# Attention and mixture of products in one kernel: storing x once in fp32, and the order of the last two products

## Chip, cores, metric

One core of one Trainium2 chip runs the whole program. The metric is device microseconds (us) for one execution; lower is better. The kernel before takes 612.06 us, the median of 3 runs (612.0 to 612.1).

## What is computed

Two stages, both fp32. The first is causal attention with a memory term, for B, H, S, D = 4, 8, 576, 64; the second is a gated feed-forward layer on the 2304 tokens (512 columns in, 1536 inside).

```
scores = q @ k.T / sqrt(64), causal
a      = softmax(scores)                       # row sums + 1e-9
local  = a @ v
p      = phi(q)                                # min(exp(q), 1) + relu(q)
mem    = (p @ M_prev) / (p @ z_prev + 1e-6)
x      = g * mem + (1 - g) * local             # g = sigmoid(beta), one per head
x      = x as [2304 tokens, 512]               # heads side by side
out    = (silu(x @ w_gate) * (x @ w_val)) @ w_out
```

## The kernel before

PE is the matrix engine. Its fp32 products are made of halves: an fp32 operand a is kept as a high part ah and a low part al = a - ah, and a product is ah*bh + ah*bl + al*bh. So every operand of a product costs a cast (high) and a subtraction (low). `act`, `dve`, `pool` and `pe` are recorders that keep each engine's work in the order in which the code is written; because a helper issues all of it, nearly every instruction carries line 84 in the profile. SP issues the DMAs in its own queue.

**Attention (lines 568 to 691).** A pair is two heads of one batch; there are 16. The loop over n, 0 to 16, is software-pipelined: pass n, here *turn n*, computes the scores and exponentials of pair n (`ps`, `pl`, `p4` tiles, with row maxima mx and row sums sm) and the transposes, memory term and values of pair n - 1; while it does so the operands of pair n + 1 are split. In a turn

- DVE reads the score banks (ISA rows, with mask and row maximum), makes the reciprocal row sums `rs` (add and reciprocal), evacuates some transposes, and does the memory term.
- POOL multiplies the exponentials by rs and 1 - g: four `ps` (after the first two row blocks) and, at the end of a pass, four `pl` and then one of `p4` (`normal`, line 443). Between them it splits the next pair: `kh`, `qh`, then `ql`, `kl` (lines 297 to 302). On POOL a turn is counted from the four `pl` scalings, which are written at the end of the pass before and run at the turn's start.
- `leave` (541) takes the finished x of a pair out of two PSUM banks (`tr` in the profile): ACT copies the high part to `xh`, DVE subtracts for the low part `xl`, in two pieces of 256 and 320 columns; the second piece is done at the start of the next turn. `d2` (553) stores `xh` and `xl` to two DRAM tensors, `xdh` and `xdl`.
- Four weight thirds are prepared beside attention (EARLY, lines 672 to 682). For the first three, the step that is written at the end of pass n runs at the start of turn n + 1. On DVE it is: turns 4 and 5, 8 and 9, 12 and 13, one op each with one input of 512 columns (clamp, then shift); turns 6, 10, 14, an op with two inputs (`wa<-we,wa`); turns 7, 11, 15, a two-input subtraction (`wgl<-wa,wgh` or like it). Turn 3 has none.

**Experts (lines 923 to 1002).** The tokens form three groups of 768, and w_gate and w_val are cut into 12 column blocks; group by block gives 36 *units*, 0 to 35. A group's x is taken as a 2 x 2 of blocks of 384 tokens by 256 columns, a11, a12, a21, a22, and in units 3 to 35 (`seven`, 879) the two products of a unit are formed from seven block products, p1, p2, p6, p7, p5, p4, p3 in this order, steps 0 to 6. Their operands are x blocks or sums of them, each with a high and a low tile (`xp1h`, `xp1l`, ...): p1 is a11, p2 is a12, p4 is a22 and p6, p7, p5, p3 are combinations, made from an fp32 copy (`xr`, with `xt` and `xm`) by four ops of 768 columns (`sums`, 749). Units 0 to 2 (`eight`) use the blocks themselves. The seven results go through two PSUM banks in turn (`bank`, 847; `s` in the profile), so that a product may start when the bank of the product before last has been read: p1 by ACT (`zp`), p2 by DVE (`zg<-s,zp`), p6 and p7 by ACT, p5 by DVE (`zv<-s,zv`), p4 by DVE (`zh<-s,zh`), p3 by DVE in `weigh`.

`weigh` (833) multiplies the gated half by the value half, ACT casts the result to `uh`, and `halves` (842) writes the subtraction `ul` at the start of the next unit. `weigh(u, 1, g2, v2)` reads two SBUF tiles; `weigh(u, 0, g1, step 6)` reads p3's bank. After each step but the first PE does one of six *lower* products of the unit before (`lower`, 803: three matmuls `tr<-...` with uh, uh, ul of one half), in the order TURN = 3, 4, 5, 0, 1, 2, the first three being those of half 1. `plan[k]` holds DVE and ACT work that is written after step k: the next unit's weight operands (`tt`, `th`, `tl`, `bh`, `bl` from `wr`, each read again from DRAM), weight thirds of later blocks in the first group (`wa`, `wol`), and in the last units of a group the x operands of the next one.

Before the experts, and at each group's end, x comes back by DMA: p1, p2, p7, p4 of the first group and p1, p2, p4 of the others as ready halves (`direct`, 745); for the sums the halves are loaded again and added to fp32 (`add`, 763, four ops of 768 columns, for the second group in units 6 to 9).

Of the kernel before, what the change touches and what calls it, by code (L numbers as in the profile page):

```python
# [9 lines left out]
F32 = mybir.dt.float32  # L10
# [34 lines left out]
def attention_moe(ctx: ExitStack, tc: tile.TileContext, qt, kt_, v, m, beta, wg, wv, wo, out):  # L45
# [9 lines left out]
    xdh = dram.tile([128, NPAIR, NT], F32, name="xdh")  # L55
    xdl = dram.tile([128, NPAIR, NT], F32, name="xdl")
# [109 lines left out]
    xs = {p: [near.tile([128, 2, N2], F32R, name=f"x{p}{part}") for part in "hl"] for p in ("p1", "p2", "p7", "p4")}  # L166

# [88 lines left out]
    with tc.tile_pool(name="sb", bufs=1, reuse_waits="tile") as sb:  # L256
# [69 lines left out]
        class Pair:  # L326
# [239 lines left out]
        ending = lambda: nothing  # L566
        copies = []
        for n in range(NP + 1):
# [10 lines left out]
            low = ending()  # L579
# [5 lines left out]
            low()  # L585
# [80 lines left out]
            ending = old.leave() if old else lambda: nothing  # L666
# [5 lines left out]
            for i, at in enumerate(EARLY):  # L672
# [13 lines left out]
        ending()()  # L686
# [7 lines left out]
    with tc.tile_pool(name="stg2", bufs=1, reuse_waits="tile") as stg2, \  # L694
# [47 lines left out]
        def block(x, t0, i, j):  # L742
            return x[:, 2 * j : 2 * j + 2, t0 + i * N2 : t0 + i * N2 + N2]

        def direct(t0, p, i, j):
            for dst, src in zip(xs[p], (xdh, xdl)):
                SP.dma_start(dst.bitcast(F32), block(src, t0, i, j))

        def sums(t0, here=False):

            got = rot(mbp, "xr", [128, 4, 2, N2], F32, 1)
            at = ((1, 0), (1, 1), (0, 0), (0, 1))
            a21, a22, a11, a12 = (got[:, n] for n in range(4))
# [299 lines left out]
```

## Time and profile before

| | us |
|---|---|
| median of 3 runs | 612.06 |
| the profiled execution | 611.38 |
| its span (first to last recorded work) | 609.6 |
| PE busy | 599.6 (98%) |
| DVE busy | 485.0 (80%) |
| ACT busy | 395.2 (65%) |
| POOL busy | 214.8 (35%) |
| attention, to the first product of the experts | 187.7 |
| one unit of the experts without a stall | 11.48 |

The shares are means over two very different halves: POOL has no work in most of the experts, and in attention it is nearly always busy. Matmuls overlap in the records, so a PE that is shown busy can still lose a few tenths of a microsecond; a loss shows as a longer distance between starts. The granted TensorE clock is full in all of the page's 40 slices.

### The profile page before, as it was taken

Reading aid. Unit: us, or ns where it says so; the run is one execution under the profiler, and the core shown is the slowest. Engines: PE = TensorE matmul, PEld = TensorE weight load, DVE = VectorE, ACT = ScalarE, POOL = GpSimd, SP = SyncE. Lnnn points to the kernel's source line nnn. Section 1 sums busy time; section 2 is a strip of 40 time slices with the busy share of each in tenths; the row PEclk is TensorE's granted clock in tenths of the full one; section 3 lists DMA queues with packets and bytes.
Section 4 is the critical chain, followed back from the end, with each engine's and each line's share of the span. In section 5 each row is a group of like instructions: output and inputs, shape, how many; then the busy total and the mean of one; then the engine's idle time right before and its main releaser. Section 6 shows DMA issues by size and latency. Waiting matters only on the chain.

```text
span 609.6 us, 11282 instructions
## 1 busy us (share of the span) xinstructions
PE 599.6 (98%) x3794; PEld 531.5 (87%) x3794; DVE 485.0 (80%) x1208; ACT 395.2 (65%) x917; POOL 214.8 (35%) x261
## 2 busy tenths in 40 slices
PE   6999999999999999999999999999999999999997
PEld 4878878778788999999899999999999999999996
DVE  6899999999988998898998665665888765665653
ACT  8788888888876777777656654454456654454442
POOL 7999999999963334334320000000000000000000
PEclk9999999999999999999999999999999999999999
DMA  8456756657337657799556622323755622332212
GB/s 250 133 159 178 255 171 204 215 179 216 141 117 277 187 182 239 239 361 282 192 175 208 217 92 70 112 96 115 232 184 177 211 100 69 107 103 69 70 35 103
DMA packets 49321, 102.46 MB, mean 168 GB/s; under 512 B 7024, under 2 KB 17136, under 8 KB 49264
## 3 DMA queue, kind: packets, MB, share of 16 engines
q1 hardware_dynamic: 48832, 101.32, 51.1%
q8 instruction: 30, 0.49, 0.3%
q10 hardware_dynamic: 432, 0.43, 0.2%
q14 instruction: 27, 0.22, 0.1%
HBM read 74.99 MB, written 26.74 MB: 167 GB/s over the span
## 4 chain that ended last, share of the span: by engine, by line
PE 96%; POOL 1%; DMA 1%; issue 0%; DVE 0%; ACT 0%; SPq 0%; ACTq 0%; DVEq 0%
PE s L84 60%; PE tr L84 36%; DMA qr<-in_qt_dram 1%; POOL ps L84 0%; POOL kl L84 0%; SPq L269 0%; ACT g L84 0%; POOL qh L84 0%; DVE rs L84 0%; ACT wa L84 0%; POOL pl L84 0%; DVE mem L84 0%; DVE pl L84 0%; SPq L560 0%; DVE pt L84 0%
## 5 line engine op out<-in xcount | busy, mean ns | idle before, releaser
L84 ACT ACTIVATE zh<-zh 128x384 f32<-128x384 f32 x33 | 17.4, 527 | 74.8 <-DVE zh L84 74.8
L84 POOL TENSOR_SCALAR pl<-pl,rs,og 128x384 f32<-128x384 f32 (+1 forms) x64 | 55.9, 886 | 9.4 <-DVE rs L84 9.4
L84 DVE TENSOR_TENSOR zv<-s,zv 128x384 f32<-128x384 f32 x33 | 18.4, 557 | 51.1 <-PE s L84 45.9
L84 PE MATMUL tr<-woh,ul 128*128 128x512 f32 x144 | 57.3, 398 | 0.0
L84 PE MATMUL tr<-woh,uh 128*128 128x512 f32 x144 | 57.0, 396 | 0.0
L84 PE MATMUL tr<-wol,uh 128*128 128x512 f32 x144 | 56.8, 394 | 0.0
L84 POOL TENSOR_SCALAR we<-we 128x512 f32<-128x512 f32 x32 | 24.9, 780 | 76.8 <-ACT we L84 76.7
L84 ACT ACTIVATE pl<-pl,mx 128x384 f32<-128x384 f32 (+1 forms) x64 | 42.3, 664 | 12.3 <-DVE mx L84 12.3
L84 PE MATMUL tr<-g,vp 128*64 128x320 f32 (+4 forms) x448 | 48.8, 360 | 0.3 <-ACT g L84 0.3
L84 DVE TENSOR_TENSOR tl<-tt,th 128x512 fp32r<-128x512 f32 x66 | 47.7, 723 | 0.0
L84 ACT CAST th<-tt 128x512 fp32r<-128x512 f32 x66 | 41.1, 622 | 9.6 <-DVE tt L84 6.3
L84 PEld LDWEIGHTS tr<-g,vp 128*64 128x64 f32 x448 | 29.4, 137 | 18.0 <-issue 2.3
L84 PE MATMUL s<-kh,qh 64*128 64x128 f32 (+4 forms) x160 | 37.2, 386 | 4.5 <-ACT kh L84 4.0
L84 ACT CAST uh<-zh 128x384 fp32r<-128x384 f32 x36 | 18.5, 513 | 32.6 <-DVE zh L84 32.3
L84 DVE TENSOR_TENSOR zg<-s,zp 128x384 f32<-128x384 f32 x33 | 18.4, 558 | 25.8 <-ACT bh L84 23.5
L84 DVE CUSTOM_DVE_ANT_0 pl<-s,maskp 128x384 f32<-128x384 f32 (+1 forms) x64 | 38.1, 615 | 0.3 <-PE s L84 0.3
L84 DVE TENSOR_TENSOR bl<-wr,bh 128x512 fp32r<-128x512 f32 x66 | 36.3, 550 | 0.0
L84 ACT CAST bh<-wr 128x512 fp32r<-128x512 f32 x66 | 33.9, 513 | 0.0
L84 PEld LDWEIGHTS tr<-woh,ul 128*128 128x128 f32 x144 | 27.1, 188 | 6.8 <-DVE ul L84 0.3
L84 ACT ACTIVATE ps<-ps,mx 128x128 f32<-128x128 f32 (+1 forms) x64 | 28.6, 453 | 6.4 <-DVE mx L84 6.4
L84 POOL TENSOR_SCALAR ps<-ps,rs,og 128x128 f32<-128x128 f32 (+1 forms) x64 | 32.0, 513 | 1.6 <-DVE rs L84 1.2
L84 DVE COPY g<-tr 128x384 f32<-128x384 f32 (+2 forms) x60 | 30.0, 518 | 2.7 <-PE tr L84 1.4
(198 smaller groups left out, 2000.4 us busy)
## 6 DMA issues: line engine op xcount, KB each, us to landing
wr<-wdr SPq DMA_DIRECT2D x24, 512.0 KB, 3.3
wraw<-in_wg_dram SPq DMA_DIRECT2D x12, 512.0 KB, 4.6
wraw<-in_wv_dram SPq DMA_DIRECT2D x12, 512.0 KB, 5.1
wraw<-in_wo_dram SPq DMA_DIRECT2D x12, 512.0 KB, 5.1
wol<-wdo SPq DMA_DIRECT2D x24, 256.0 KB, 2.8
woh<-wdo SPq DMA_DIRECT2D x24, 256.0 KB, 3.1
qr<-in_qt_dram SPq DMA_DIRECT2D x15, 384.0 KB, 3.2
vp<-in_v_dram SPq DMA_DIRECT2D x16, 320.0 KB, 4.1
```

The source lines that it names most:

```text
L84: ins = getattr(eng, name)(*args, **kw)
```

## The change

x is kept once, in fp32. `leave` copies both pieces to one tile `xo` on ACT, and one store a pair goes to one DRAM tensor `xd`; `give`, `d2` and the `xl` subtractions are gone. Where x is used it is loaded as fp32 and split there:

- First group: p1, p2, p7, p4 are loaded into their low tiles in turns 6, 8, 10, 12, and at the end of the two turns after each, ACT casts one half of the tile to the high tile; the subtraction that leaves the low part in place is written a pass later, so that DVE runs the eight of them at the starts of turns 9 to 16, behind the weight op, where there is one.
- `sums` loads four fp32 blocks and adds nothing; of its eight ops of 768 columns four are left.
- Second and third group: p1, p2, p4 are split from `xr` too, p1 and p2 in the group's last unit before them, p4 in the first unit of the group.

In the experts `weigh` reads p3's bank first and the two SBUF tiles second, in all units but the last; the lower products follow in the order 0 to 5 instead of TURN, so that the half that is weighed first is used first; the six lower products after the last unit keep TURN.

```diff
-    xdh = dram.tile([128, NPAIR, NT], F32, name="xdh")
-    xdl = dram.tile([128, NPAIR, NT], F32, name="xdl")
+    xd = dram.tile([128, NPAIR, NT], F32, name="xd")
...
+    where = dict(p1=(0, 0), p2=(0, 1), p7=(1, 0), p4=(1, 1))
+
+    def x_block(t0, i, j):
+        return xd[:, 2 * j : 2 * j + 2, t0 + i * N2 : t0 + i * N2 + N2]
...
-            def give(self, t0, src):
-                c = slice(t0 * 128, t0 * 128 + src.shape[1])
-                act.copy(self.xh[:, c], src)
-                return lambda: dve.tensor_tensor(self.xl[:, c], src, self.xh[:, c].bitcast(F32), op=ALU.subtract)
...
             def leave(self):
                 first, rest = self.av
-                self.xh = rot(sb, "xh", [128, 576], F32R, NX)
-                self.xl = rot(sb, "xl", [128, 576], F32R, NX)
-                self.give(0, first[:, 0:256])()
+                x = rot(sb, "xo", [128, 576], F32, NX)
+                act.copy(x[:, 0:256], first[:, 0:256])
 
                 def ending():
-                    low = self.give(2, rest[:, 0:320])
-                    return lambda: (low(), self.d2())
+                    act.copy(x[:, 256:576], rest[:, 0:320])
+                    SP.dma_start(xd[:, self.pr, self.b * S : self.b * S + S], x)
 
                 return ending
-
-            def d2(self):
-                for dst, src in ((xdh, self.xh), (xdl, self.xl)):
-                    SP.dma_start(dst[:, self.pr, self.b * S : self.b * S + S], src.bitcast(F32))
...
+            for p, at in zip(("p1", "p2", "p7", "p4"), (6, 8, 10, 12)):
+                high, low = xs[p]
+                if n == at:
+                    SP.dma_start(low.bitcast(F32), x_block(ORDER[0], *where[p]))
+                for k in range(2):
+                    if n == at + 1 + k:
+                        act.copy(high[:, k], low[:, k].bitcast(F32))
+                    if n == at + 2 + k:
+                        dve.tensor_tensor(low[:, k], low[:, k].bitcast(F32), high[:, k].bitcast(F32), op=ALU.subtract)
...
-        def direct(t0, p, i, j):
-            for dst, src in zip(xs[p], (xdh, xdl)):
-                SP.dma_start(dst.bitcast(F32), block(src, t0, i, j))
...
-        def sums(t0, here=False):
+        def sums(t0):
 
             got = rot(mbp, "xr", [128, 4, 2, N2], F32, 1)
-            at = ((1, 0), (1, 1), (0, 0), (0, 1))
             a21, a22, a11, a12 = (got[:, n] for n in range(4))
             s1, s = (rot(mbp, name, [128, 2, N2], F32, 1) for name in ("xt", "xm"))
-            tmp = (s, s1)
-            mix = dict(p6=s, p7=a11, p5=s1, p3=a12)
-
-            def load(n):
-                for dst, src in ((got[:, n], xdh), (tmp[n % 2], xdl)):
-                    ld = SP.dma_start(dst, block(src, t0, *at[n]))
-                    follow(ld, last[DVE], "the loads that come before go first", mybir.DependencyClass.Sync)
-
-            def add(n):
-                if here:
-                    h, l = (x.bitcast(F32) for x in xs[("p7", "p4", "p1", "p2")[n]])
-                    dve.tensor_tensor(got[:, n], h, l, op=ALU.add)
-                    return
-                dve.tensor_tensor(got[:, n], got[:, n], tmp[n % 2], op=ALU.add)
-                if n + 2 < 4:
-                    load(n + 2)
+            mix = dict(p1=a11, p2=a12, p6=s, p7=a11, p5=s1, p4=a22, p3=a12)
+
+            def begin():
+                for n, at in enumerate(((1, 0), (1, 1), (0, 0), (0, 1))):
+                    SP.dma_start(got[:, n], x_block(t0, *at))
 
             tt = lambda out, a, b, op: (lambda: dve.tensor_tensor(out, a, b, op=op))
-            work = [lambda n=n: add(n) for n in range(4)] + [
-                tt(s1, a21, a22, ALU.add), tt(s, s1, a11, ALU.subtract), tt(a12, a12, s, ALU.subtract),
-                tt(a11, a11, a21, ALU.subtract),
-            ]
-            return lambda: (load(0), load(1)), work, mix
+            return begin, [
+                tt(s1, a21, a22, ALU.add), tt(s, s1, a11, ALU.subtract),
+                tt(a11, a11, a21, ALU.subtract), tt(a12, a12, s, ALU.subtract),
+            ], mix
...
             rest(5)
-            weigh(u, 1, g2, v2)
-            weigh(u, 0, g1, step(6, "p3", False))
+            ps = step(6, "p3", False)
+            for i, g, v in ((1, g2, v2), (0, g1, ps)) if final else ((0, g1, ps), (1, g2, v2)):
+                weigh(u, i, g, v)
             rest(6)
             return u
...
-                    if left == 0:
-                        plan[2].append(due[7])
-                        plan[3] += spreads(mix, ("h", "p6"))
-                        plan[4] += spreads(mix, ("l", "p6"), ("h", "p7"))
-                        plan[6] += spreads(mix, ("l", "p7"))
-                        arrive = [
-                            (1, spreads(mix, ("h", "p5"))), (2, spreads(mix, ("l", "p5"))),
-                            (3, spreads(mix, ("h", "p3"))), (4, spreads(mix, ("l", "p3"))),
-                        ]
+                if left == 3:
+                    begin, due, mix = sums(follows)
+                    plan[3].append(begin)
+                if left == 1:
+                    plan[2].append(due[0])
+                    plan[5].append(due[1])
+                if left == 0:
+                    plan[1] += spreads(mix, ("h", "p1"))
+                    plan[2] += spreads(mix, ("l", "p1"), ("h", "p2"))
+                    plan[3] += [due[2]] + spreads(mix, ("l", "p2"), ("h", "p6"))
+                    plan[4] += spreads(mix, ("l", "p6"), ("h", "p7")) + [due[3]]
+                    plan[6] += spreads(mix, ("l", "p7"))
+                    arrive = [
+                        (0, spreads(mix, ("h", "p5"))), (1, spreads(mix, ("l", "p5"), ("h", "p4"))),
+                        (2, spreads(mix, ("l", "p4"), ("h", "p3"))), (3, spreads(mix, ("l", "p3"))),
+                    ]
             down = [] if before is None else [
-                lambda j=j, before=before: lower(*before, j) for j in (range(2 * nj) if n <= PLAIN else TURN)
+                lambda j=j, before=before: lower(*before, j) for j in range(2 * nj)
             ]
...
-                before = (unit, seven(ready.pop(n), down, plan, (0, 2, 4) if f else (3, 5, 6)))
-            if not end and left == 0:
-                direct(follows, "p1", 0, 0)
-                direct(follows, "p2", 0, 1)
-                direct(follows, "p4", 1, 1)
+                before = (unit, seven(ready.pop(n), down, plan, (0, 2, 4) if f else (3, 5, 6), n == len(units) - 1))
```

On DVE, at the start of turn 11, the order before is this (`ph` is phi(q), `tr` the bank with x, `s` the score banks):

```order
L84 SCALAR_TENSOR_TENSOR ph_240<-qe_241,ph_240 128x640
L84 TENSOR_TENSOR rs_279<-sm_152,tiny 128x1
L84 RECIPROCAL rs_279<-rs_279 128x1
L84 TENSOR_TENSOR xl_567<-tr_298,xh_566 128x256
L84 TENSOR_TENSOR wgl_1014<-wa_1453,wgh_1013 128x512
L84 ISA ps_271,mx_255<-s_161,maskp 128x128
L84 ISA mx_255 128x1
L84 ISA ps_273,mx_255<-s_162,maskp 128x128
L84 ISA mx_255 128x1
L84 TENSOR_TENSOR xl_567<-tr_303,xh_566 128x320
```

And after:

```order
L83 SCALAR_TENSOR_TENSOR ph_239<-qe_240,ph_239 128x640
L83 TENSOR_TENSOR rs_278<-sm_151,tiny 128x1
L83 RECIPROCAL rs_278<-rs_278 128x1
L83 TENSOR_TENSOR wgl_998<-wa_1430,wgh_997 128x512
L83 TENSOR_TENSOR xp2l<-xp2l,xp2h 128x384
L83 ISA ps_270,mx_254<-s_160,maskp 128x128
L83 ISA mx_254 128x1
L83 ISA ps_272,mx_254<-s_161,maskp 128x128
L83 ISA mx_254 128x1
L83 ISA ps_274,mx_254<-s_152,maskp 128x256
```

Both `xl` are gone, one of them from behind the second pair of score reads, and an `xp2l` subtraction of two SBUF tiles stands directly behind `wgl`.

On DVE, at the end of unit 10 and the first drains of unit 11 (the second `zg` row reads p2's bank in unit 11), before:

```order
L84 TENSOR_TENSOR zh_2647<-s_154,zh_2647 128x384
L84 TENSOR_TENSOR tl_2788<-tt_2786,th_2787 128x512
L84 TENSOR_TENSOR xr_2587<-xr_2587,xm_2589 128x768
L84 SCALAR_TENSOR_TENSOR zh_2647<-zv_2909,zh_2647 128x384
L84 SCALAR_TENSOR_TENSOR zg_2602<-s_153,zg_2602 128x384
L84 TENSOR_TENSOR ul_2665<-zh_2647,uh_2664 128x384
L84 TENSOR_TENSOR ul_2625<-zg_2602,uh_2624 128x384
L84 TENSOR_TENSOR zg_2681<-s_153,zp_2908 128x384
```

After:

```order
L83 TENSOR_TENSOR zh_2610<-s_153,zh_2610 128x384
L83 TENSOR_TENSOR tl_2749<-tt_2747,th_2748 128x512
L83 TENSOR_TENSOR xm_2550<-xt_2549,xr_2548 128x768
L83 SCALAR_TENSOR_TENSOR zg_2567<-s_152,zg_2567 128x384
L83 SCALAR_TENSOR_TENSOR zh_2610<-zv_2870,zh_2610 128x384
L83 TENSOR_TENSOR ul_2589<-zg_2567,uh_2588 128x384
L83 TENSOR_TENSOR ul_2627<-zh_2610,uh_2626 128x384
L83 TENSOR_TENSOR zg_2643<-s_152,zp_2869 128x384
```

The product that reads p3's bank (`zg<-s,zg`) now goes ahead of the one that doesn't (`zh<-zv,zh`), and so do its low half and, with other operands, the 768-column op.

On DVE, in unit 11, from the second weight subtraction to the drain of p4's bank (`zh<-s,zh`), before:

```order
L84 TENSOR_TENSOR xr_2587<-xr_2587 128x768
L84 TENSOR_TENSOR wol_2807<-wa_2040,woh_2806 128x512
L84 TENSOR_TENSOR tl_2905<-tt_2786,th_2904 128x512
L84 TENSOR_TENSOR tt_2786<-wr_2811,tt_2786 128x256
L84 TENSOR_TENSOR zv_2909<-s_154,zv_2909 128x384
L84 TENSOR_TENSOR bl_2907<-wr_2811,bh_2906 128x256
L84 TENSOR_TENSOR xp6l<-xm_2589,xp6h 128x384 x2
L84 TENSOR_TENSOR zh_2742<-s_153,zh_2742 128x384
L84 TENSOR_TENSOR tl_2905<-tt_2786,th_2904 128x512
```

After:

```order
L83 TENSOR_TENSOR xp1l<-xr_2548,xp1h 128x384 x2
L83 TENSOR_TENSOR wol_2768<-wa_2015,woh_2767 128x512
L83 TENSOR_TENSOR tl_2866<-tt_2747,th_2865 128x512
L83 TENSOR_TENSOR tt_2747<-wr_2772,tt_2747 128x256
L83 TENSOR_TENSOR xr_2548<-xr_2548 128x768
L83 TENSOR_TENSOR xp2l<-xr_2548,xp2h 128x384 x2
L83 TENSOR_TENSOR zv_2870<-s_153,zv_2870 128x384
L83 TENSOR_TENSOR bl_2868<-wr_2772,bh_2867 128x256
L83 TENSOR_TENSOR xp6l<-xm_2550,xp6h 128x384 x2
L83 TENSOR_TENSOR xr_2548<-xr_2548,xm_2550 128x768
L83 TENSOR_TENSOR zh_2703<-s_152,zh_2703 128x384
L83 TENSOR_TENSOR tl_2866<-tt_2747,th_2865 128x512
```

Four subtractions (`xp1l`, `xp2l`, two each) and a second op of 768 columns now stand ahead of `zh<-s,zh`.

## Rows read from the trace of the kernel before

**Rows 1.** The page's first part: busy us (share of span) and instructions.
```profile
PE 599.6 (98%) x3794; PEld 531.5 (87%) x3794; DVE 485.0 (80%) x1208; ACT 395.2 (65%) x917; POOL 214.8 (35%) x261
```
**Rows 2.** Windows view, turns 4 to 14: window, length, busy of each engine, PEclk, DMA, GB/s.
```profile
47.06:168.11 121.05, 121.05 (x1115) 97.36 (x1113) 113.49 (x430) 103.51 (x294) 116.54 (x143) 1.00 0.62 195
```
**Rows 3.** Timeline of POOL: start, us, instruction [idle before <-releaser].
```profile
35.89 3.24 POOL L84 TENSOR_SCALAR pl<-pl,rs,og 128x384 f32<-128x384 f32 x4 [0.41 <-DVE rs L84]
...
47.06 3.46 POOL L84 TENSOR_SCALAR pl<-pl,rs,og 128x384 f32<-128x384 f32 x4 [0.52 <-DVE rs L84]
...
57.97 3.46 POOL L84 TENSOR_SCALAR pl<-pl,rs,og 128x384 f32<-128x384 f32 x4 [0.41 <-DVE rs L84]
...
112.90 3.73 POOL L84 TENSOR_SCALAR pl<-pl,rs,og 128x384 f32<-128x384 f32 x4 [0.41 <-DVE rs L84]
...
124.05 3.73 POOL L84 TENSOR_SCALAR pl<-pl,rs,og 128x384 f32<-128x384 f32 x4 [0.41 <-DVE rs L84]
...
128.56 0.67 POOL L84 TENSOR_SCALAR kh<-kr 128x576 fp32r<-128x576 f32 x1
...
133.35 1.43 POOL L84 TENSOR_TENSOR kl<-kr,kh 128x576 fp32r<-128x576 f32 x1
```
**Rows 4.** Timeline of DVE in turns 3 and 11.
```profile
37.69 0.49 DVE L84 TENSOR_TENSOR xl<-tr,xh 128x320 fp32r<-128x320 f32 x1
...
124.77 0.42 DVE L84 TENSOR_TENSOR xl<-tr,xh 128x256 fp32r<-128x256 f32 x1
...
125.11 0.71 DVE L84 TENSOR_TENSOR wgl<-wa,wgh 128x512 fp32r<-128x512 f32 x1
...
128.86 0.38 DVE L84 TENSOR_TENSOR rs<-sm,tiny 128x4 f32<-128x4 f32 x1
...
134.45 0.34 DVE L84 TENSOR_TENSOR rs<-sm,tiny 128x4 f32<-128x4 f32 x1
```
**Rows 5.** Waits of ACT: waited for, us in total, times, longest.
```profile
ACT xh L84 <- PE tr L84: 5.7, 12, 0.5
```
**Rows 6.** Chain of waits, units 7, 11 and 12: start, us, piece.
```profile
267.29 2.33 PE s L84 x12
...
314.20 2.23 PE s L84 x12
...
325.83 2.08 PE s L84 x12
```
**Rows 7.** Timeline of PE, unit 7, the step from p1 to p2.
```profile
268.00 0.34 PE L84 MATMUL s<-xp1h,bl 128*128 128x384 f32 x1
268.31 0.44 PE L84 MATMUL s<-xp2h,bh 128*128 128x384 f32 x1
268.59 0.34 PE L84 MATMUL s<-xp2l,bh 128*128 128x384 f32 x1
268.77 0.34 PE L84 MATMUL s<-xp2h,bl 128*128 128x384 f32 x1
```
**Rows 8.** Timeline of DVE and ACT, units 10 and 11.
```profile
313.18 0.95 DVE L84 TENSOR_TENSOR xr<-xr,xm 128x768 f32<-128x768 f32 x1
...
316.54 0.56 DVE L84 TENSOR_TENSOR zg<-s,zp 128x384 f32<-128x384 f32 x1 [0.28 <-PE s L84]
...
322.20 0.92 ACT L84 CAST xp6h<-xm 128x384 fp32r<-128x384 f32 x2
...
322.75 1.03 DVE L84 TENSOR_TENSOR xp6l<-xm,xp6h 128x384 fp32r<-128x384 f32 x2
...
323.69 0.55 DVE L84 TENSOR_TENSOR zh<-s,zh 128x384 f32<-128x384 f32 x1
...
326.72 0.55 DVE L84 TENSOR_TENSOR ul<-zh,uh 128x384 fp32r<-128x384 f32 x1
```
**Rows 9.** Timeline of PE, the first matmul of units 12 and 24.
```profile
325.67 0.34 PE L84 MATMUL s<-xp1h,bh 128*128 128x384 f32 x1
...
463.43 0.34 PE L84 MATMUL s<-xp1h,bh 128*128 128x384 f32 x1
```
**Rows 10.** Timeline of DVE, unit 23 and the start of unit 24.
```profile
459.52 0.56 DVE L84 TENSOR_TENSOR zv<-s,zv 128x384 f32<-128x384 f32 x1 [1.19 <-PE s L84]
...
461.26 0.55 DVE L84 TENSOR_TENSOR zh<-s,zh 128x384 f32<-128x384 f32 x1
...
464.34 0.55 DVE L84 TENSOR_TENSOR ul<-zh,uh 128x384 fp32r<-128x384 f32 x1
```

More of the change, by code (lines that the diff above doesn't have):

```diff
@@ L565, in attention_moe @@
         nothing = lambda *args: None
-        ending = lambda: nothing
+        ending = nothing
         copies = []
@@ L578, in attention_moe @@
                 old.turns()
-            low = ending()
+            ending()
             while copies:
@@ L584, in attention_moe @@
             reads[0](1)
-            low()
             if n == 0:
@@ L665, in attention_moe @@
                     cur.weighed(((4, 0),))
-            ending = old.leave() if old else lambda: nothing
+            ending = old.leave() if old else nothing
             if n + 2 < NP:
@@ L877, in eight, with seven @@
             return u
-        def seven(w, down, plan, away_at):
+        def seven(w, down, plan, away_at, final):
             def step(n, p, start, before=None):
@@ L915, in attention_moe @@
         first = units[0][0]
-        for p, i, j in (("p1", 0, 0), ("p2", 0, 1), ("p7", 1, 0), ("p4", 1, 1)):
-            direct(first, p, i, j)
         before = None
@@ L948, in attention_moe @@
                 if f == 0:
-                    _, due, mix = sums(t0, True)
-                    for k, some_ in enumerate(((0,), (1,), (2, 4), (3,))):
-                        plan[k] += [due[i] for i in some_]
+                    begin, due, mix = sums(t0)
+                    begin()
+                    plan[2].append(due[0])
+                    plan[3].append(due[1])
                 if f == 1:
-                    for k in range(3):
-                        plan[k].append(due[5 + k])
-                    for k, p in ((0, "p5"), (2, "p6")):
-                        plan[k] += spreads(mix, ("h", p))
+                    for k, i, p in ((0, 2, "p5"), (2, 3, "p6")):
+                        plan[k] += [due[i]] + spreads(mix, ("h", p))
                         plan[k + 1] += spreads(mix, ("l", p))
@@ L963, in attention_moe @@
                 follows = ORDER[ORDER.index(t0) + 1]
-                if t0 == first and left in (5, 4, 3):
-                    if left == 5:
-                        begin, due, mix = sums(follows)
-                        begin()
-                    plan[5].append(due[5 - left])
-                if not plain:
-                    if left == 3 and t0 != first:
-                        begin, due, mix = sums(follows)
-                        plan[3].append(begin)
-                    if left == 2:
-                        for k, work in zip((5,), due[3:]) if t0 == first else zip((2, 4, 6), due):
-                            plan[k].append(work)
-                    if left == 1:
-                        for k, work in zip((1, 3, 5), due[4:]) if t0 == first else zip((1, 2, 4, 6), due[3:]):
-                            plan[k].append(work)
-                    if left == 0:
-                        plan[2].append(due[7])
-                        plan[3] += spreads(mix, ("h", "p6"))
-                        plan[4] += spreads(mix, ("l", "p6"), ("h", "p7"))
-                        plan[6] += spreads(mix, ("l", "p7"))
-                        arrive = [
-                            (1, spreads(mix, ("h", "p5"))), (2, spreads(mix, ("l", "p5"))),
-                            (3, spreads(mix, ("h", "p3"))), (4, spreads(mix, ("l", "p3"))),
-                        ]
```

5 lines of the change are left out of this document (2 added, 3 removed).

## The prediction

> **What bounds the kernel now.** The page's first part comes first: PE is busy 599.6 of 609.6 us [rows 1]. Matmuls overlap, so short waits hide inside that busy time, and the two halves have to be read one by one.
>
> *Attention.* Turns 4 to 14 of the loop over pairs last 121.05 us; PE counts as busy throughout, POOL is busy 116.54 us [rows 2]. A turn begins on POOL with the four scalings of pl, and before them POOL waits 0.41 us for rs [rows 3]. 11 x 0.41 = 4.51, and 116.54 + 4.51 = 121.05: POOL waits for nothing else. So a turn is as long as POOL's work plus 0.41 us, and the others keep POOL's pace. Now see what lengthens that work. The four scalings take 3.24 us in turn 3, 3.46 in turns 4 and 5, 3.73 in turns 10 and 11, and the turns follow: 47.06 to 57.97 is 10.91 us, 112.90 to 124.05 is 11.15 [rows 3]. By the code, what differs at this place is the weight preparation on DVE: none in turn 3, a one-input op of 512 columns in turn 4, a two-input op in turns 10 and 11, as wgl with 0.71 us [rows 4]. The other way round, rs of 128.86 ends at 129.24 with kh (129.23), that of 134.45 at 134.79 with kl (134.78) [rows 3, 4]. DVE ops with both inputs in SBUF and POOL's ops take turns. The xl subtractions are in every turn; they read PSUM and one SBUF tile, and POOL's 3.24 us of turn 3 (35.89 to 39.13) contain one at 37.69 [rows 3, 4]: they do not hold POOL up.
>
> The Trainium skill, "SBUF — State Buffer", section "Who interferes with whom", says the same in general: a VectorE instruction with two SBUF inputs contends with a GpSimd instruction that reads SBUF, one with a single SBUF input outside the 2-port modes does not, and whoever is first holds the port for its whole instruction. The rows agree on who contends, and not quite on the price: by the rule the 0.71 us of wgl would cost POOL 0.71, the rows show 0.49. With the rule's price the sum below would be 0.5 us higher. It speaks against this change, which puts two-input subtractions where one input was PSUM.
>
> *Experts.* The chain of waits is PE's own matmuls. Its pieces of 12 matmuls (p1 and p2) take 2.08 us, but 2.33 in units 7 to 10 and 2.23 in unit 11 [rows 6] (the first of the long ones, that of unit 11 and a short one): 4 x 0.25 + 0.15 = 1.15 us. Inside, the first matmul of p2 starts 0.31 us after its predecessor, not 0.17 [rows 7]. Its bank was last read by the unit before, by the zg product, which stands on DVE behind a 768-column add (0.95 us, as at 313.18) [rows 8] and the other product.
>
> **The change part by part.**
>
> *Stores.* In turns 2 to 16 DVE loses both xl, 0.34 us (124.77 to the next start at 125.11) and about 0.40 [rows 4], and SP one store. Neither is in POOL's work or its 0.41 us, so I take no gain; rival 1 has the other end. ACT copies the same bits as fp32: nothing.
>
> *Splitting x for the first group.* Eight casts come to ACT in turns 7 to 14, between the two copies of x. There ACT waits 5.7 us in 12 turns, 0.48 each [rows 5]; a cast of 384 columns costs 0.46 (two in 0.92) [rows 8]. In turns 10 and 14 a weight op fills that gap already and ACT is 0.46 later; it waits on DVE next. Nothing.
>
> Eight subtractions come to DVE at the starts of turns 9 to 16, from two SBUF tiles. Their like, xp6l, takes 1.03 for two and its follower starts 0.94 after [rows 8], so 0.47 each in the queue. They stand directly behind the weight op (the first order listing). A lone op of 0.71 costs POOL 0.49 (3.73 - 3.24), so 0.22 of one is hidden; an op that follows at once has nothing left to hide in. Low end 0.55 - 0.22 = 0.33, high end 0.55, and 0.47 is nearest to what is in the queue. Turns 9 to 14: 6 x 0.47 = **+2.8** (2.0 to 3.3). In turns 15 and 16 no further pair is split and POOL's work is short: +0.1 (0 to 0.3).
>
> *Loads.* Four loads in turns 6 to 12 in place of eight; later four per group for fourteen. No DMA is in the chain of either half. The loads of a group now wait in SP's queue until DVE and ACT have read the tile, with weight loads behind them; I count 0, up to 0.3.
>
> *Experts, units 6 to 10.* The adds of high and low are gone. Unit 10 keeps a 768-column op there, but the zg product, which frees the bank, now goes ahead of the other one. The stalls go: **-1.15** (at least -0.9). Elsewhere there was no such stall, and the new order of the two products has nothing to give. The last unit keeps its order.
>
> *Unit 11, where the second group is made ready.* p1, p2 and p4 came by DMA as halves; now they are split. Ahead of DVE's zh add (the drain of p4's bank) stand four more subtractions, 4 x 0.47 = 1.88, and a 768-column op that was in unit 10, 0.87: 2.75 us. DVE's visible wait there is 0.28 [rows 8]; the rest, 2.45 to 2.5, is delay. The zh add ended at 323.69 + 0.55 = 324.24, and p1 of the next unit started at 325.67 [rows 8, 9]: 1.43 of room. PE stalls 2.45 - 1.43 = 1.0. Then the first ul: it ended near 327.27, now 329.7; PE wants it as third matmul of the first lower product, 2.08 + 0.46 after p1, at 326.67 + 2.54 = 329.2. Another 0.45. **+1.45** (0.5 to 2.4: at the low end DVE has more short waits to fill, at the high end nothing gives).
>
> *Unit 23* has the same work without weight words. DVE waits 1.19 us before zv [rows 10], so of 2.75 some 1.5 remains. Room up to p1: 463.43 - 461.81 = 1.6 [rows 9, 10], no stall. The first ul, 464.89 before, comes at 466.4; wanted at 463.43 + 2.54 = 465.97: **+0.4** (0 to 1).
>
> *Sum:* 2.8 + 0.1 - 1.15 + 1.45 + 0.4 = +3.6 us. The profiled execution took 611.38 us (span 609.6); 611.38 + 3.6 = 615.0. The median of the runs, 612.06, is 0.68 higher, so **615.7 us**.
>
> **The rivals.**
>
> *1. DVE sets the pace of attention.* DVE is busy 113.49 of 121.05 us [rows 2]. If the xl were on the path, turns 4 to 8 would gain 0.74 each and turns 9 to 14 0.74 - 0.47 = 0.27: 3.7 + 1.6 = 5.3, and the sum would be -5.3 + 0.7 = -4.6: 607.5 us. A smaller form, 0.1 to 0.2 a turn from PE's short waits, gives 610 to 611. Against it: POOL's account closes without DVE's share, and turn 3, with all its xl, has the shortest scalings.
>
> *2. The subtractions cost POOL nothing* because POOL's lateness is made up, if DVE, now earlier elsewhere, has rs ready sooner and the 0.41 us shrink. Then only the experts count: +0.7, 612.8; with unit 11 half covered, 612.0. Against it: rs becomes ready after kl has begun (134.45 against 133.35) [rows 3, 4], so it would have to come 1.1 us sooner.
>
> *3. Turns lose more than POOL's work.* Turn 3 lasts 11.17 us (35.89 to 47.06), though its scalings are the shortest; by its work it should last 10.69. If such half microseconds come to three or four of turns 9 to 14, because DVE's queue is now later at the start of the turn and its rs meets POOL's next op, the time is 617.5 to 618. For it: turn 3 shows that it occurs. Against: once in 11 turns.
>
> *4. The reordered products decide nothing:* with the adds gone the stalls would go anyway. It changes no time; it says which edit has the -1.15.
>
> **How the numbers follow.** The forecast has 0.6, rival 1 0.12, rival 2 0.18, rival 3 0.1. A measurement tells 0.2%, 1.2 us, from no change: 610.8 to 613.3. The forecast's low ends together are 2.0 - 1.15 + 0.5 + 0 = +1.35, 613.4, just above that; its high ends 3.3 + 0.3 + 0.3 - 0.9 + 2.4 + 1 = +6.4, which need not meet, and two thirds of the way up from the middle to there is 617.5. Slower: the forecast but for 0.03 and rival 3, 0.67. Same: rival 2 without its fast edge and a little of the forecast, 0.19. Faster: rival 1 and that edge, 0.14. To leave out no more than 0.2 the range reaches down into rival 2: 611.5 to 617.5.
>
> **What would show it.** POOL's four scalings should take 3.9 to 4.2 us in turns 9 to 14 and stay at 3.46 and 3.73 in turns 4 to 8; turn starts 11.3 to 11.6 us apart there. If they stay at 10.9 to 11.15, that step is wrong. The pieces of 12 matmuls in units 7 to 11 should all take 2.08. In unit 12 PE should stand before p1 and before the third matmul of the first lower product; in unit 24 before the latter alone. If turns 4 to 8 get shorter, DVE had a part in the pace, and rival 1 is right.

## The result, and the profile after

The changed kernel takes 615.88 us (median of 6 runs) beside 612.03 us of the kernel before on the same chip; the ratio is 1.0067, 95% interval 1.0054 to 1.0080. It is slower, and 615.7 was forecast. The profiled execution took 615.79 us with a span of 614.0, against 611.38 and 609.6.

The page's first part, busy us, share of the span and instructions, answers to [rows 1]:

```profile
PE 600.1 (98%) x3794; PEld 529.6 (86%) x3794; DVE 473.6 (77%) x1184; ACT 400.9 (65%) x937; POOL 218.3 (36%) x261
```

DVE does 11.4 us less work than before and the kernel is slower: DVE's total was not what bounds it. The windows view of the same eleven turns as in [rows 2] (window, length, busy of PE, PEld, DVE, ACT, POOL, PEclk, DMA share, GB/s):

```profile
46.91:170.45 123.54, 122.88 (x1115) 97.74 (x1113) 113.07 (x414) 106.31 (x301) 118.05 (x144) 1.00 0.51 155
```

The eleven turns take 123.54 us, 2.49 more, and POOL is busy 1.51 more. POOL's timeline at the starts of turns 4, 5, 8, 9, 10 and 11 and the first scalings of ps in turn 4 (start, us, instruction, [idle before]) answers to [rows 3]:

```profile
46.91 3.39 POOL L83 TENSOR_SCALAR pl<-pl,rs,og 128x384 f32<-128x384 f32 x4 [0.52 <-DVE rs L83]
...
52.84 1.96 POOL L83 TENSOR_SCALAR ps<-ps,rs,og 128x128 f32<-128x128 f32 x4 [0.40 <-ACT ph L83]
...
58.22 3.40 POOL L83 TENSOR_SCALAR pl<-pl,rs,og 128x384 f32<-128x384 f32 x4 [0.50 <-DVE rs L83]
...
91.68 3.38 POOL L83 TENSOR_SCALAR pl<-pl,rs,og 128x384 f32<-128x384 f32 x4 [0.41 <-DVE rs L83]
...
102.50 3.78 POOL L83 TENSOR_SCALAR pl<-pl,rs,og 128x384 f32<-128x384 f32 x4 [0.41 <-DVE rs L83]
...
113.69 4.03 POOL L83 TENSOR_SCALAR pl<-pl,rs,og 128x384 f32<-128x384 f32 x4 [0.41 <-DVE rs L83]
...
125.15 4.04 POOL L83 TENSOR_SCALAR pl<-pl,rs,og 128x384 f32<-128x384 f32 x4 [0.41 <-DVE rs L83]
```

Before, the scalings of turn 9 were these:

```profile
102.04 3.46 POOL L84 TENSOR_SCALAR pl<-pl,rs,og 128x384 f32<-128x384 f32 x4 [0.41 <-DVE rs L84]
```

Two things are to be seen. From turn 9 on the four scalings take 3.78 and 4.03 us where they took 3.46 and 3.73 (that row and [rows 3]): that is the forecast step. And turn 4 lasts 11.31 us (46.91 to 58.22) instead of 10.91, with *shorter* scalings and a new wait of 0.40 before ps: that was not forecast.

The stretches side by side, from POOL's pl starts in attention and from the first matmuls of units in the experts (us; the forecast is the term of the prediction):

| stretch | before | after | difference | forecast |
|---|---|---|---|---|
| to the start of turn 4 | 47.06 | 46.91 | -0.15 | 0 |
| turns 4 and 5 | 21.78 | 22.64 | +0.86 | 0 |
| turns 6 to 8 | 33.20 | 32.95 | -0.25 | 0 |
| turns 9 to 14 | 66.07 | 67.95 | +1.88 | +2.8 |
| from there to the first product of the experts | 19.62 | 19.87 | +0.25 | +0.1 |
| unit 1 | 12.52 | 13.26 | +0.74 | 0 |
| stalls at p2 in units 7 to 11 | 1.15 | 0 | -1.15 | -1.15 |
| units 11 and 12, without that | 22.96 | 24.51 | +1.55 | +1.45 |
| units 23 and 24 | 22.96 | 23.54 | +0.58 | +0.4 |
| sum | | | +4.31 | +3.6 |

The other units take the same time in both, 11.48 us from unit 3 on.

In the experts, the chain of waits in units 10 and 11 (start, us, piece) shows that the pieces [rows 6] at 2.33 have lost their stall. The piece of 30 matmuls is the one of 12, two lower products and two more products run together, 2.08 + 2 x 0.70 + 2 x 1.04 = 5.56 us:

```profile
305.05 5.56 PE s L83 x30
...
316.53 2.10 PE s L83 x12
...
327.52 0.87 DVE xr L83
328.39 0.47 DVE zh L83
```

The last two are the forecast of unit 11: zh, the drain of p4's bank, stands behind a 768-column op. It begins 11.86 us after the unit's first piece (328.39 - 316.53), where it was 9.49 [rows 6, 8]: 2.37 later, 2.45 to 2.5 were forecast. On PE (timeline, the first matmul of p3 and of unit 12's p1, and the third matmul of the first lower products of units 12 and 24 with the one ahead of it):

```profile
326.31 0.45 PE L83 MATMUL s<-xp3h,bh 128*128 128x384 f32 x1
...
328.91 0.45 PE L83 MATMUL s<-xp1h,bh 128*128 128x384 f32 x1 [0.58 <-DVE zh L83]
...
331.36 0.40 PE L83 MATMUL s<-wol,uh 128*128 128x512 f32 x1
331.85 0.50 PE L83 MATMUL s<-woh,ul 128*128 128x512 f32 x1
...
469.67 0.40 PE L83 MATMUL s<-wol,uh 128*128 128x512 f32 x1
470.18 0.50 PE L83 MATMUL s<-woh,ul 128*128 128x512 f32 x1
```

PE stands before p1 and then before the matmul that needs the first ul (0.49 and 0.51 us after its predecessor instead of 0.24), where the prediction put it.

Unit 1 was not forecast. The chain of waits from the end of attention on:

```profile
192.16 0.61 POOL we L83
192.77 6.07 DMA xr<-xd
198.83 1.15 issue
199.98 0.06 DVE xt L83
200.04 0.81 issue
200.85 0.56 DVE zh L83
201.41 0.04 issue
201.46 5.84 PE s L83 x30
```

The loads of x for the sums are let go at 192.77 and land 6.07 us later, in a stretch where the DMA engines are full (windows view, 192 to 202 us: DMA share 1.04, 388 GB/s). DVE's first sum, xt, waits for them, and zh of unit 0, which drains the bank for the second product of unit 1, is queued behind xt. Before, those sums were made from halves that lay in SBUF.

### The profile page after: what moved, and what is told of

Its sections match the earlier page's. It is cut to its first block, busy times and chain, and to the rows that moved or that the text cites. A ratio compares the mean times of both kernels' runs of the same rounds, so it can differ in the third digit from the quotient of the medians.

```text
span 614.0 us, 11191 instructions
## 1 busy us (share of the span) xinstructions
PE 600.1 (98%) x3794; PEld 529.6 (86%) x3794; DVE 473.6 (77%) x1184; ACT 400.9 (65%) x937; POOL 218.3 (36%) x261
## 4 chain that ended last, share of the span: by engine, by line
PE 88%; DVE 5%; DMA 2%; ACT 2%; issue 1%; POOL 1%; SPq 0%; ACTq 0%; DVEq 0%; POOLq 0%
PE s L83 54%; PE tr L83 34%; DMA xr<-xd 1%; DMA qr<-in_qt_dram 1%; DVE rs L83 1%; DMA kr<-in_kt_dram 0%; DVE xr L83 0%; ACT g L83 0%; DVE zh L83 0%; DVE mem L83 0%; DVE zg L83 0%; DVE xp7l L83 0%; DVE xp6l L83 0%; DVE pl L83 0%; DVE tt L83 0%
## 5 line engine op out<-in xcount | busy, mean ns | idle before, releaser
L83 POOL TENSOR_SCALAR pl<-pl,rs,og 128x384 f32<-128x384 f32 (+1 forms) x64 | 58.1, 921 | 9.6 <-DVE rs L83 9.6
L83 POOL TENSOR_SCALAR we<-we 128x512 f32<-128x512 f32 x32 | 26.7, 836 | 74.1 <-ACT we L83 73.8
L83 ACT CAST uh<-zg 128x384 fp32r<-128x384 f32 x36 | 18.5, 514 | 37.8 <-DVE zg L83 37.7
L83 DVE SCALAR_TENSOR_TENSOR zg<-s,zg 128x384 f32<-128x384 f32 x36 | 20.0, 556 | 17.4 <-PE s L83 17.4
```

The source lines that it names most:

```text
L83: ins = getattr(eng, name)(*args, **kw)
```

## Experiments

Kernels without a ratio ran once; a few tenths between such times mean nothing, and their traces are what counts.

### The order of the last two products, undone and alone

Undone in the changed kernel (a_old_order), and put alone into the kernel before (b_new_order):

```
-            ps = step(6, "p3", False)
-            for i, g, v in ((1, g2, v2), (0, g1, ps)) if final else ((0, g1, ps), (1, g2, v2)):
-                weigh(u, i, g, v)
+            weigh(u, 1, g2, v2)
+            weigh(u, 0, g1, step(6, "p3", False))
...
-    for j in range(2 * nj)
+    for j in (range(2 * nj) if n <= PLAIN else TURN)
```

> The changed kernel with only the order of the last two products and of the lower products put back. If the order is what frees p2's bank (my step), units 7 to 11 show PE stalls at p2 again, 0.1 to 0.25 us each, wherever a 768-column op stands in the unit before (in this plan units 10 and 11), so 0.2 to 0.5 us in all, and the rest of the 1.15 us stays away since the adds are gone. By rival 4 nothing comes back: all pieces of 12 matmuls stay at 2.08. Attention is unchanged in either case (experts start at 190.3).

> The kernel before with only the new order of the last two products and of the lower products. The adds of high and low stay. If the order frees the bank, the five pieces of 12 matmuls in units 7 to 11 go from 2.33 and 2.23 to 2.08: -1.15 us, 610.9. By rival 4 (the adds are the cause and order decides nothing) it stays at 612.0, with 2.33.

Undone: 616.13 us. Units 7 to 10 stay at 11.48 us; the chain of waits there and in unit 11:

```profile
270.44 2.08 PE s L83 x12
...
281.92 2.08 PE s L83 x12
...
316.36 2.10 PE s L83 x12
```

No stall comes back in units 7 to 11. Units 12 and 24 lose 0.69 and 0.68 instead of 0.49 and 0.50, now at p2's first matmul.

Alone: 610.66 us beside 611.62, ratio 0.9983 (0.9973 to 0.9992). The chain in units 7 and 8:

```profile
267.46 5.56 PE s L84 x30
...
278.94 5.59 PE s L84 x30
```

The stalls go here too, but for 0.03 us a unit; the experts are 1.06 us shorter. So either edit removes the 1.15 us, and with both the second has nothing left to do: in this change rival 4 is right, the order decides only 0.38 us in units 12 and 24, and by itself it is worth a microsecond.

### The eight subtractions beside attention, left out

```
-                    if n == at + 2 + k:
-                        dve.tensor_tensor(low[:, k], low[:, k].bitcast(F32), high[:, k].bitcast(F32), op=ALU.subtract)
```

> The changed kernel without the eight subtractions beside attention: the low halves of the first group's x are left as the whole x, so the output is not the reference's. Theory (two-input DVE work holds POOL up): the four scalings of pl in turns 9 to 14 fall from 3.78 and 4.04 to 3.39 and 3.65, each of these turns by 0.39, turns 15 and 16 by little; experts start 2.3 to 2.6 us earlier, at 187.7 to 188.0, and the time is about 613.4. The long turns 4 and 5 (11.31 and 11.33) stay. Rival (DVE's queue, not POOL, is the path): the scalings keep their length and PE's turns fall by 0.47.

614.86 us. POOL's timeline, pl of turns 9, 10, 12 and 13, and ps of turn 12:

```profile
102.96 3.37 POOL L83 TENSOR_SCALAR pl<-pl,rs,og 128x384 f32<-128x384 f32 x4 [0.41 <-DVE rs L83]
...
113.72 3.64 POOL L83 TENSOR_SCALAR pl<-pl,rs,og 128x384 f32<-128x384 f32 x4 [0.42 <-DVE rs L83]
...
135.79 3.37 POOL L83 TENSOR_SCALAR pl<-pl,rs,og 128x384 f32<-128x384 f32 x4 [0.41 <-DVE rs L83]
...
141.71 1.95 POOL L83 TENSOR_SCALAR ps<-ps,rs,og 128x128 f32<-128x128 f32 x4 [0.40 <-ACT ph L83]
...
147.11 3.38 POOL L83 TENSOR_SCALAR pl<-pl,rs,og 128x384 f32<-128x384 f32 x4 [0.51 <-DVE rs L83]
```

The scalings fall by 0.40, as expected, and turns 9, 10, 11 and 14 by 0.40 to 0.43. But turns 12 and 13 get *longer* without the subtraction, 11.32 and 11.30 instead of 11.20 and 11.19, with the wait of 0.40 before ps that turn 4 has. Together -1.44 in turns 9 to 14 instead of -2.4; a subtraction costs 0.40 where it costs anything. Turns 9 to 14 still last 66.51 us, 0.44 more than before: of the +1.88 of the table only 1.44 is the subtractions', the rest comes with xl's going (next section).

### xl left out of the kernel before

```
-                return lambda: dve.tensor_tensor(self.xl[:, c], src, self.xh[:, c].bitcast(F32), op=ALU.subtract)
+                return lambda: None
...
-                for dst, src in ((xdh, self.xh), (xdl, self.xl)):
+                for dst, src in ((xdh, self.xh), (xdl, self.xh)):
```

> The kernel before without the subtractions for xl (both stores take xh, so the low half of x is wrong). Theory: attention gains next to nothing from it. By what the changed kernel's trace shows, the scalings of pl get 0.07 shorter, so turns 6 to 14 gain 0.07 each, but kh then ends just before rs is ready in turns 4 and 5 and these become 0.4 longer: experts start between 187.2 and 188.2 (187.73 before). By rival 1 (DVE sets the pace) each of turns 4 to 14 is 0.3 to 0.74 shorter, and the experts start at 180 to 184.

> The kernel before without the xl subtractions again (the low half of x is wrong), timed: open is whether taking xl away costs time or whether turn 4 of the kernel before is itself at the edge, so that the single profile misled. Theory (the shorter scalings let kh end just before rs arrives, in turns 4, 5, 12 and 13): 0.5 to 1.2 us slower than the kernel before, ratio 1.001 to 1.002, the spread of the kernel before wider than its own. By the prediction's step: no change. By rival 1: 5 us faster.

Both profiles agree to 0.05 us: turns 4, 5, 12 and 13 last 11.3 us, the others of 4 to 14 0.05 to 0.11 less than before. The first product of the experts starts at 188.80 in the first, 1.07 later than in the profile of before. Timed, the ratio is 1.0006 (0.9997 to 1.0014; 612.29 beside 611.89): no difference that can be told. Rival 1 wanted 5 us less. What lies between the two answers is seen in turn 4, kh and qh on POOL and rs on DVE. Before:

```profile
51.30 0.67 POOL L84 TENSOR_SCALAR kh<-kr 128x576 fp32r<-128x576 f32 x1
51.94 0.73 POOL L84 TENSOR_SCALAR qh<-qr 128x640 fp32r<-128x640 f32 x1
...
51.92 0.10 DVE L84 TENSOR_TENSOR rs<-sm,tiny 128x4 f32<-128x4 f32 x1
```

After:

```profile
51.07 0.68 POOL L83 TENSOR_SCALAR kh<-kr 128x576 fp32r<-128x576 f32 x1
51.71 0.73 POOL L83 TENSOR_SCALAR qh<-qr 128x640 fp32r<-128x640 f32 x1
...
51.78 0.67 DVE L83 TENSOR_TENSOR rs<-sm,tiny 128x4 f32<-128x4 f32 x1
52.48 0.18 DVE L83 RECIPROCAL rs<-rs 128x4 f32<-128x4 f32 x1
```

rs adds 1e-9 to four row sums, an op of 0.10 us with two SBUF inputs. Before, it arrives 0.05 us ahead of kh's end (51.97) and gets in at once. After, it arrives 0.03 us behind kh's end (51.75): qh has the turn, rs waits it out (0.67 us), and ps waits for rs. The row of ps at 52.84 names ph as what ended its wait. But ps starts 0.18 us after the end of rs's reciprocal (52.66), just as pl at 47.06 before follows its own by 0.18, and without the add (below) the wait is gone.

So the scalings that got 0.07 us shorter without xl cost 0.4 us a turn; why they got shorter is not shown. Before stands at this edge itself: in the profiles of b_two_sbuf and b_two_psum below, whose turns 3 to 8 are the same code, rs arrives 0.03 to 0.04 ahead of kh's end, misses, and turns 4 and 5 take 11.37 to 11.38 us. So the +0.86 of the table is partly luck of the profile of before; of the profiles with the add, turns 4 and 5 were long in every one without xl, and in two of four with it. The 0.05 us alone does not decide either. In turn 3 of the profile of before rs also arrives 0.05 us ahead of kh's end (40.58), and it misses:

```profile
39.89 0.69 POOL L84 TENSOR_SCALAR kh<-kr 128x576 fp32r<-128x576 f32 x1
...
40.53 0.75 DVE L84 TENSOR_TENSOR rs<-sm,tiny 128x4 f32<-128x4 f32 x1
```

### Two more subtractions, from SBUF or from PSUM

In the kernel before, behind the first xl of turns 9 to 16; the control has `first[:, 0:256]` (the PSUM bank) in place of the first input:

```
                 self.give(0, first[:, 0:256])()
+                if 7 <= self.n <= 14:
+                    junk = rot(sb, "junk", [128, 256], F32, 1)
+                    for _ in range(2):
+                        dve.tensor_tensor(junk[:, 0:256], self.xh[:, 0:256].bitcast(F32), self.xl[:, 0:256].bitcast(F32), op=ALU.subtract)
```

> The kernel before with two more DVE subtractions of 128x256 behind the first xl at the starts of turns 9 to 16, each from two SBUF tiles into a tile that nobody reads. Theory (two-input SBUF work on DVE holds POOL up): 0.33 us each in the queue, so the four scalings of pl grow by 0.5 to 0.7 us in turns 9 to 14 and so do the turns; experts start about 3 to 4 us later, near 191.3. Rival (POOL is free of it, DVE's queue is the path): the scalings stay at 3.46 and 3.73.

> The control of the run with two SBUF inputs: the same two DVE subtractions of 128x256 in the same place, but one input is the PSUM bank that holds x. Theory: the scalings of pl stay within 0.1 of 3.46 and 3.73 and the experts start at 187.7 to 188.5. If DVE's queue were the path, these two would cost as much as the SBUF ones, 3 to 4 us.

621.69 and 619.91 us, far more than expected of either. POOL's pl at turn 9 with SBUF inputs:

```profile
103.69 3.89 POOL L84 TENSOR_SCALAR pl<-pl,rs,og 128x384 f32<-128x384 f32 x4 [0.41 <-DVE rs L84]
```

and with PSUM, pl and ps of turn 9:

```profile
103.58 3.37 POOL L84 TENSOR_SCALAR pl<-pl,rs,og 128x384 f32<-128x384 f32 x4 [0.41 <-DVE rs L84]
...
109.85 1.95 POOL L84 TENSOR_SCALAR ps<-ps,rs,og 128x128 f32<-128x128 f32 x4 [0.77 <-ACT qe L84]
```

The scalings do what the theory says: 3.45 becomes 3.89 with SBUF inputs, and 3.37 with PSUM ones. But the two ops also make DVE later: in turn 9 rs of ps comes 5.62 us after the start of pl with SBUF inputs and 5.77 with PSUM ones, where before it came after 4.65. POOL waits for it in turns 9 to 14, 0.76 to 1.00 us with PSUM inputs (turns of 11.7 to 12.2 us) and 0.40 to 1.09 with SBUF ones (11.8 to 12.7); where qe is named as releaser, as above, the reciprocal of rs again ends 0.17 us before ps.

So most of what these runs lost, some 8 of 10 us, is DVE's queue, and only the 1.8 us between them is what the SBUF inputs add: up to that rs DVE has little slack, 0.26 us in turn 9 before (rs at 106.69, kh ends at 106.95). In the change rs of turn 9 comes after 4.79 us, hardly later: the two xl, 0.74 us a turn, left DVE's queue as the subtraction of 0.47 came in. The prediction counted xl's going as nothing; by these sums it was worth having as cover for the subtraction, though no run has the subtraction and xl together.

### rs without its add

A row sum holds an exp(0), so 1e-9 is below its last bit, and the reciprocal can be taken at once. First in ps alone, then everywhere, in the changed kernel; then everywhere in the kernel before, with the new order of products:

```
-                if by is None:
-                    dve.tensor_tensor(rs, self.sm[:, c : c + n], tiny[:, 0:n], op=ALU.add)
-                else:
+                if by is not None:
...
-                    dve.reciprocal(rs, rs)
+                    dve.reciprocal(rs, self.sm[:, c : c + n])
```

> The changed kernel with rs of the first two row blocks (the ps scalings) taken without the add of 1e-9, all other adds kept. Theory (turns 3, 4 and 5 are long because this add, with two SBUF inputs, comes just after kh has ended and has to wait until qh is done): these three turns fall from 11.15, 11.31 and 11.33 to about 10.75, 10.9 and 10.9, the others stay, POOL keeps its 0.41 us before pl; experts start 1.2 us earlier, at 189.1. Rival (the long turns come from something else, such as ACT or a load): no turn changes.

> The changed kernel with rs taken as the reciprocal of the row sum itself, the add of 1e-9 (a DVE op with two SBUF inputs) left out; a row sum holds an exp(0), so 1e-9 is below its last bit. Theory (the add waits for POOL's running op and POOL then waits for rs): turns 3, 4 and 5 lose their extra 0.4 us, POOL's wait before pl goes from 0.41 to 0.1 or less in every turn, so 14 turns get 0.3 to 0.4 shorter; experts start 5 to 6.5 us earlier, at 184 to 185.5, time 609.5 to 611. Rival (POOL's 0.41 us is the way from ACT's last exponential through rs, whatever rs is made of): only the add's own 0.15 us go, 2 us in all.

> The kernel before with the new order of the last two products and with rs without the add of 1e-9. Theory: 610.7 of the new order, less 13 turns of 0.3 to 0.4 and 0.4 for turn 3, so 605 to 606.5. Rival (the wait is the way through rs): 608.5.

In ps alone (614.69 us): turns 3, 4 and 5 fall from 11.14, 11.31 and 11.33 to 10.25, 10.78 and 10.75, POOL's 0.41 us before pl stay in nearly all turns. At the start of turn 3 this execution is 1.5 us late, as is the one of a_units below (1.4), whose attention is unchanged; from there to pl of turn 16 it is 2.2 us shorter. The long turns came from this add.

Everywhere (611.96 us): POOL's 0.41 us vanish, turns 4 to 8 take 10.6 to 10.8 us, the experts start at 186.30, 4.0 earlier, where 5 to 6.5 were expected. One turn went the other way, 12.97 us. DVE's ph and POOL's four pl there:

```profile
130.86 3.96 DVE L83 SCALAR_TENSOR_TENSOR ph<-qe,ph 128x640 f32<-128x640 f32 x1
```

```profile
131.33 2.82 POOL L83 TENSOR_SCALAR pl<-pl,rs,og 128x384 f32<-128x384 f32 x4
```

ph, two SBUF inputs, 0.80 us elsewhere, is ready at 130.86 while kl runs, and ends at 134.82, 0.67 after the last of pl (134.15). At four boundaries between POOL's ops POOL went on and DVE did not. In the kernel before, ph goes into the gap that POOL's wait for rs leaves: in turn 4 it starts at 46.80, pl at 47.06.

In the kernel before: 606.73 us beside 611.78, ratio 0.9925 (0.9911 to 0.9938), the fastest of all here; its runs reach from 605.35 to 609.13. In its profile, that of the run at 605.35, no ph was held for as long. Whether one was in the run at 609.13 is not shown.

### The experts' queue on DVE

In the changed kernel, xt behind zh in unit 0, and the two ops of 768 columns of units 11 and 23 a unit earlier, into tiles of their own:

```
-                    plan[2].append(due[0])
-                    plan[3].append(due[1])
+                    plan[3] += due[0:2]
...
-                tt(a11, a11, a21, ALU.subtract), tt(a12, a12, s, ALU.subtract),
+                tt(d7, a11, a21, ALU.subtract), tt(d3, a12, s, ALU.subtract),
...
-                    plan[2].append(due[0])
-                    plan[5].append(due[1])
+                    for k, work in zip((1, 2, 4, 5), due):
+                        plan[k].append(work)
```

> The changed kernel with two edits in the experts: in unit 0 the first 768-column add (xt) is written after zh's drain, and for the second and third group the two ops of 768 columns that stand in the last unit write tiles of their own, so that they can be done one unit earlier. Theory: unit 1's bank wait came from zh queued behind xt, which waits for the load of x; unit 1 goes from 13.26 back to 12.52 us. In units 11 and 23 1.74 us less stands ahead of zh, and of the 1.54 and 0.58 us of stall most goes: units 11, 12, 23 and 24 take 11.5 to 11.7. Together 2.3 to 2.9 us less in the experts. Rival (the wait in unit 1 is PE's or the load's own, not DVE's order; the stall in unit 11 is from the four subtractions alone): unit 1 stays at 13.2, unit 11 loses at most half. Attention is unchanged.

614.58 us. Unit 1 takes 12.52 us, units 11, 12, 23 and 24 11.81, 11.48, 11.48 and 11.48: 2.53 us less. The rest, 0.33, is a p2 stall: its bank waits for zg behind the ops that now stand in unit 10. The time of the run shows only half of it, since its attention ends 1.3 us later than in the profile after; the kernel before, run beside it, took 613.07 us.

### All mends together

> The changed kernel with all mends together: rs without the add of 1e-9 everywhere, xt behind zh in unit 0, and the two ops of 768 columns one unit earlier. Theory: the parts add up. Experts 2.53 us shorter than in the changed kernel (unit 11 keeps 0.33 of stall), attention 4.0 us shorter where one turn is still held up by ph (as the changed kernel without the add showed), 6.5 where none is: 615.9 - 6.5 = 609.4, or 606.9. So x stored once can come below the kernel before, by 0.4 to 0.8%, but not below the kernel before with the new order and without the add (606.7). Rival (the parts share a cause): not under 610.5.

615.26 us (609.54 to 616.75), ratio to the kernel before 1.0038 (1.0015 to 1.0061): neither theory. The experts did keep their 2.5 us. In the profiled execution two turns were locked as above and took some 15 us. The windows view around the first (window, length, busy of PE, PEld, DVE, ACT, POOL, PEclk):

```profile
122.00:124.00 2.00, 2.00 (x23) 1.86 (x24) 2.00 (x1) 0.93 (x3) 1.94 (x3) 1.00 0.82 230
124.00:126.00 2.00, 0.28 (x3) 0.04 (x1) 2.00 (x7) 0.02 (x1) 1.15 (x1) 1.00 0.97 320
126.00:127.00 1.00, 0.11 (x1) 0.11 (x1) 1.00 (x7) 1.00 (x4) 1.00 (x3) 1.00 0.89 349
127.00:128.00 1.00, 1.00 (x6) 1.00 (x7) 0.78 (x2) 1.00 (x6) 0.69 (x1) 0.58 0.12 48
128.00:130.00 2.00, 2.00 (x12) 1.77 (x13) 0.81 (x5) 1.96 (x6) 0.13 (x1) 0.50 0.04 8
130.00:132.00 2.00, 2.00 (x17) 1.58 (x14) 1.66 (x6) 0.79 (x3) 2.00 (x5) 0.86 0.00 0
```

DVE has one instruction in 122 to 124: ph, waiting. PE then stands for 2.61 us, and when it goes on the granted clock is 0.58 and 0.50 for some 3 us; 0.50 is the lower of its two levels, 1.2 of 2.4 GHz. By PE's first score matmuls the turn lasts 15.1 us where the next one lasts 10.66: 2.61 of standing and, by the clock column, 1.7 of slow matmuls behind it. Taking POOL's wait away is a gamble in this kernel. It seems to be lost more often in the changed kernel, whose 12 mended runs lie between 609.54 and 616.75; that its two-input subtractions are the cause is not shown.

## Why the prediction came out right, and where it did not

- **The sum** (+3.6 forecast, +4.31 by the table, 3.85 between the medians) is nearer than its parts, and that is partly luck: by the runs the subtractions of turns 9 to 14 cost 1.44 us and not 2.8, while unit 1 (+0.74) and xl's going (+1.0 and +1.3 over turns 4 to 14 in the two profiles without it, less on the clock) were counted as nothing. The profile of before lies 0.65 under its median, perhaps in part by the edge in turns 4 and 5. In rival 3's time three to four half microseconds on 615.7 make 617.1 to 617.6; the prediction's 617.5 to 618 is some 0.4 too high, which changes nothing here.
- **POOL as the bound of attention** held in turns 6 to 14: a turn is POOL's work and its wait before pl. It did not hold in turns 4 and 5 after the change, where POOL also waits for DVE's rs, nor with the two added DVE ops, nor where ph was locked out.
- **Eight subtractions, +2.8.** The mechanism is shown by the scalings (3.38 to 3.78, back to 3.37 when left out, and by the SBUF and PSUM pair). The size of one is 0.40 where 0.47 was taken, inside its bounds of 0.33 to 0.55, but in turns 12 and 13 it is below nothing, since the longer scalings carry kh's end past rs. 1.88 came against before, under the term's low end of 2.0, and of it only 1.44 is theirs. So the scalings took 3.78 and 4.03 where 3.9 to 4.2 was the sign, and the turns 11.19 to 11.47 where 11.3 to 11.6 was.
- **xl's going, 0.** On the clock this stands (1.0006, 0.9997 to 1.0014). By the trace it is two things that were missed: scalings 0.07 shorter, and turns 4 and 5 falling over an edge. The prediction had the same op in turn 11, where rs comes 0.37 us ahead of kh's end [rows 3, 4], and read it as proof that the two engines take turns; how near the other turns come to missing, 0.05 in turn 4, was not asked. The first of the two also spoils one of its signs: turns 6 to 8 did get shorter, by 0.25 together, which was to show rival 1. They follow POOL's scalings, and rival 1 wanted 0.74 in each.
- **Rival 3** named the right meeting, rs with POOL's next op, and turn 3 as its example; it came in turns 4 and 5 instead of 9 to 14, because POOL was earlier and not because DVE was later (from the start of pl, rs came after 4.86 us before and 4.87 after, kh's end after 4.91 and 4.84).
- **Loads, 0 up to 0.3.** This step failed: +0.74 in unit 1. The prediction looked for DMAs in the chain of the kernel before, where the sums of the first group took halves that were in SBUF; the new load has a reader, xt, with a bank's drain queued behind it. Which op stands behind the first reader was the question to ask.
- **Units 7 to 11, -1.15** exact; that the order of the products frees the bank is true by itself (-1.06) and superfluous beside the other edit.
- **Units 11 and 23, +1.45 and +0.4**: +1.55 and +0.58, at the matmuls named. Two small waits were missed: 0.2 us before p3 of unit 11, and 0.08 in unit 23, before p1 of unit 24.

## What to carry to other kernels

Where two engines exclude each other, a turn's length depends on which of two events comes first, and an op made shorter can cost more than it saves: read how far apart the two ends are, here 0.05 us, before counting a removed op as nothing. A wait may be the gap that another engine lives on; removing it is worth trying (0.75% here, with the new order of the products, which alone gave 0.17%) but wants many runs, not one profile. Before a transfer is counted as free, look at what is queued behind its first reader.

## What the runs showed of the hardware that was not expected

A DVE op with two SBUF inputs that waits for POOL need not get in at the next boundary between POOL's ops: in three turns ph was held for 3.96, 3.99 and 3.95 us while POOL ran kl and four scalings back to back. In all three ph arrived about 0.5 us before kl's end; but three others that arrived as early (0.51 to 0.56) in the profile of a_no_add got in when kl ended, so what decides it stays open. The Trainium skill, "SBUF — State Buffer", section "Who interferes with whom", calls the port pair that the two engines share an exclusive lock, and says of DVE's 2-port modes that who issues first has the pair for the whole instruction and the other is blocked; the traces agree for one instruction (rs behind qh, 0.67 us), and show beyond it that the blocked one can lose several times running. Open too is the 1.15 us between the landing of x's loads and xt.
